# More three-pass blocks, eps in the Gram matrix, and small products spaced apart, in an attention and SwiGLU kernel

## The chip, the cores and the metric

The kernel runs on one core of a Trainium2 chip. The metric is the device time of one execution in microseconds, the median of several; executions of one kernel agree within some 0.3%. Every result was correct. Times of different jobs are compared through their ratios to the kernel before, which ran in each.

## The reference

```python
# x: 4 batches of 12416 tokens x 128 channels; 32 inducing points
h = mab(I, x); out = mab(x, h)        # mab: softmax attention, a = exp(s - max) / (sum + 1e-9), a @ kv
# then per token, 49664 tokens, d_ff = 1536
rms = sqrt(mean(out * out) + 1e-6); xn = out / rms * rms_g
g = xn @ w_gate; v = xn @ w_val
y = (g * sigmoid(g) * v) @ w_out
```

The second attention's division and the RMS norm need not both be done: with e the unnormalized weights and l their sum, out / rms is e·h / sqrt(mean((e·h)²) + 1e-6·l²). The kernel gets the mean from the Gram matrix of h, as eᵀ(hhᵀ)e / 128.

## The kernel before

Tokens go through the feed-forward part in units of up to 512, and each unit in twelve blocks of 128 columns of d_ff. A block is a gate matmul and a value matmul (into banks `gv`), a silu on ScalarE, a product `u` on VectorE, and a projection that adds to `acc`. Some blocks project in three reduced-precision passes instead of one full fp32 matmul; ScalarE and GpSimd prepare their operands:

```python
    def three(j, t):                      # what a three-pass block adds
        nc.scalar.activation(hi, v, AF.Copy, scale=1.0 - 2.0 ** -13)
        nc.gpsimd.tensor_tensor(out=lo, in0=v, in1=hi.bitcast(F32), op=ALU.subtract)
        ...                               # one block later:
        nc.scalar.activation(hs[:, 0:T], hi.bitcast(F32), AF.Copy, scale=2.0 ** -12)
        nc.gpsimd.tensor_tensor(out=d, in0=hs[:, 0:T], in1=lo.bitcast(F32), op=ALU.subtract)
```

Every 48 blocks a "seam" prepares the weights of the next four units, a step at a time between blocks. Its last step, `split`, turns the weights, rounds them (a cast) and takes the rest (a subtraction).

```python
        def split():
            aT = work.tile([P, 512], F32, name="aT", tag="work")
            nc.vector.transpose(out=aT[rows, 0:w], in_=sc[b][rows, cols2[s]])
            ...
            nc.vector.tensor_copy(out=hi[rows, 0:w], in_=aT[rows, 0:w])
            nc.vector.tensor_tensor(out=lo[rows, 0:w], in0=aT[rows, 0:w], in1=hi[rows, 0:w].bitcast(F32), op=ALU.subtract)
...
                # block of each seam step: turn_a, sum_l, square, turn_z, scale, apply, split
                j = ((14, 14, 17, 18, 21, 21, 33) if k else (32, 32, 33, 33, 34, 34, 37))[i]
```

All small products (scores, sums, the Gram product `square`) share one PSUM bank, `mm`. Before each exp, which occupies ScalarE (one instruction of 2.88 us at the first of a batch, two in 3.04 us at the second at 449 us, each with a table load of 1.28 us), the kernel holds projections back so that TensorE has work meanwhile.

## Time and profile before

| | before |
|---|---|
| median (range) | 1716.28 us (1715.45 to 1718.89) |
| profiled span, granted clock | 1713.4 us, 0.995 |
| TensorE busy | 98% |
| three-pass blocks | 337 of 1200 |

The prediction below shows the lines of the page and of the timeline, and how they are read. Two names recur. "Spacing" is the time from the start of one value matmul to the next, that is, the time of one block on TensorE. A "releaser" is what ended a wait.

### The profile page before, as it was taken

The page shows a single profiled execution, that of the slowest core. Times are in us where ns is not written, and L with a number is a line of the kernel's source. Part 1 is how long each engine was busy: PE and PEld are TensorE (multiplying, and loading weights), DVE is VectorE, ACT ScalarE, POOL GpSimd, SP SyncE. Part 2 cuts the span into 40 slices and gives each one's busy share as a digit, 9 for nine tenths or more (in the row PEclk, how much of TensorE's full clock was granted, in tenths as well). Part 3 has the DMA queues.
Part 4 walks back from the last instruction along what each step waited for, and adds up shares of the span by engine and source line. Part 5 has one row for each costly group of instructions (what it writes and reads, how often), then busy time and mean ns, then how long its engine had stood idle before and what let it go on. Part 6 is the DMA issues. An engine that isn't in the chain of part 4 may idle for free.

```text
span 1713.4 us, 23133 instructions
## 1 busy us (share of the span) xinstructions
PE 1676.4 (98%) x6791; PEld 1033.1 (60%) x6791; DVE 1203.1 (70%) x2086; ACT 1145.1 (67%) x2052; POOL 1029.4 (60%) x808
## 2 busy tenths in 40 slices
PE   9899999999999999999999999999999999999998
PEld 7545555655566656565556656566556666666666
DVE  4867876777677777667767787666767666766665
ACT  4346667665777676665667767766577777777775
POOL 0316663656477665465747766466647767767764
PEclk9899999999999999999999999999999999999999
DMA  6344433524343232434334313163211212121111
GB/s 248 87 68 74 73 76 61 120 64 73 60 79 68 48 61 56 102 73 93 64 55 82 67 34 81 31 131 75 59 30 32 39 31 37 31 38 34 35 36 24
DMA packets 389357, 112.64 MB, mean 66 GB/s; under 512 B 365136, under 2 KB 369776, under 8 KB 386672
## 3 DMA queue, kind: packets, MB, share of 16 engines
q1 hardware_dynamic: 388944, 111.02, 32.2%
q8 instruction: 54, 0.88, 0.2%
q14 instruction: 71, 0.58, 0.1%
q10 hardware_dynamic: 288, 0.15, 0.0%
HBM read 53.95 MB, written 27.00 MB: 47 GB/s over the span
## 4 chain that ended last, share of the span: by engine, by line
PE 88%; DVE 4%; ACT 4%; issue 2%; POOL 1%; DMA 1%; DVEq 0%; ACTq 0%; POOLq 0%
PE acc L555 43%; PE gv L604 15%; PE gv L602 15%; PE u L568 5%; PE u L570 4%; PE mm L300 2%; DVE u L608 1%; PE mm L483 1%; ACT silu L606 1%; PE mm L357 1%; DMA xn<-in_x_dram 1%; PE acc L177 1%; ACT sc L416 1%; ACT L606 1%; ACT sc L329 0%
## 5 line engine op out<-in xcount | busy, mean ns | idle before, releaser
L608 DVE TENSOR_TENSOR u<-silu,gv 128x512 f32<-128x512 f32 (+2 forms) x1200 | 787.8, 665 | 457.7 <-ACT silu L606 409.0
L606 ACT ACTIVATE silu<-gv 128x512 f32<-128x512 f32 (+2 forms) x1200 | 698.8, 584 | 491.2 <-PE gv L602 377.4
L555 PE MATMUL acc<-u,wo 128*128 128x512 f32 (+2 forms) x1726 | 863.1, 584 | 1.7 <-DVE u L608 1.0
L602 PE MATMUL gv<-a,sg 128*128 128x512 f32 (+2 forms) x1200 | 788.4, 657 | 7.7 <-ACT silu L606 5.3
L590 POOL TENSOR_TENSOR xn<-u,xn 128x512 fp32r<-128x512 f32 (+2 forms) x337 | 433.6, 1287 | 403.0 <-ACT xn L589 398.0
L604 PE MATMUL gv<-a,sv 128*128 128x512 f32 (+2 forms) x1200 | 469.4, 391 | 2.9 <-ACT silu L606 1.8
L595 POOL TENSOR_TENSOR xn<-hs,xn 128x512 fp32r<-128x512 f32 (+2 forms) x337 | 422.7, 1254 | 59.7 <-issue 15.9
L555 PEld LDWEIGHTS acc<-u,wo 128*128 128x128 f32 x1726 | 317.5, 189 | 112.9 <-issue 47.2
L602 PEld LDWEIGHTS gv<-a,sg 128*128 128x128 f32 x1200 | 227.2, 189 | 222.2 <-issue 151.0
L604 PEld LDWEIGHTS gv<-a,sv 128*128 128x128 f32 x1200 | 227.3, 189 | 216.0 <-issue 119.7
L589 ACT ACTIVATE xn<-u 128x512 fp32r<-128x512 f32 (+2 forms) x337 | 206.4, 612 | 20.7 <-DVE u L608 20.4
L594 ACT ACTIVATE hs<-xn 128x512 f32<-128x512 f32 (+2 forms) x337 | 206.3, 612 | 0.4 <-POOL xn L595 0.4
L568 PE MATMUL u<-xn,xn 128*128 128x512 f32 (+2 forms) x337 | 142.4, 422 | 0.0
L555 PE MATMUL acc<-xn,xn 128*128 128x512 f32 (+2 forms) x337 | 131.3, 390 | 2.8 <-POOL xn L595 2.8
L570 PE MATMUL u<-xn,xn 128*128 128x512 f32 (+2 forms) x337 | 130.6, 388 | 0.0
L498 POOL TENSOR_TENSOR rs<-ms,mhalf 128x16 f32<-128x16 f32 (+2 forms) x28 | 75.6, 2699 | 24.9 <-DVE ms L496 24.9
L568 PEld LDWEIGHTS u<-xn,xn 128*128 128x128 f32 x337 | 63.2, 188 | 27.2 <-issue 15.8
L490 POOL TENSOR_TENSOR z<-z,sc 128x512 f32<-128x512 f32 (+2 forms) x27 | 32.4, 1201 | 78.5 <-DVE z L489 47.3
L555 PEld LDWEIGHTS acc<-xn,xn 128*128 128x128 f32 x337 | 63.2, 188 | 18.1 <-POOL xn L595 4.3
L570 PEld LDWEIGHTS u<-xn,xn 128*128 128x128 f32 x337 | 63.4, 188 | 16.6 <-issue 4.3
L561 DVE STREAM_TRANSPOSE o<-o 128x512 f32<-128x512 f32 (+2 forms) x97 | 67.7, 698 | 3.4
L560 DVE TENSOR_TENSOR o<-acc,o 128x512 f32<-128x512 f32 (+2 forms) x97 | 64.7, 667 | 2.6 <-PE acc L555 2.2
(159 smaller groups left out, 789.1 us busy)
## 6 DMA issues: line engine op xcount, KB each, us to landing
out_dram<-o SPq DMA_DIRECT2D x320, 64.0 KB, 2.0
xT<-in_x_dram SPq DMA_DIRECT2D x60, 256.0 KB, 4.3
xn<-in_x_dram SPq DMA_DIRECT2D x60, 256.0 KB, 4.8
a<-hi SPq DMA_DIRECT2D x160, 64.0 KB, 2.0
a<-lo SPq DMA_DIRECT2D x158, 64.0 KB, 2.0
w<-w SPq DMA_DIRECT2D x22, 256.0 KB, 3.2
xn<-in_x_dram SPq DMA_DIRECT2D x5, 1024.0 KB, 10.6
out_dram<-o SPq DMA_DIRECT2D x64, 60.0 KB, 2.0
```

The costliest lines, as they stand in the source:

```text
L498: nc.gpsimd.tensor_tensor(out=rs, in0=ms, in1=mhalf[rows, 0:n], op=ALU.pow)
L555: nc.tensor.matmul(acc[:, 0:T], lhsT, rhs, start=st["left"] == NJ, stop=st["left"] == 1)
L568: nc.tensor.matmul(ups[:, 0:T], w[:, i, :], hi, start=st["k"] == nk, stop=False)
L570: nc.tensor.matmul(ups[:, 0:T], w[:, NK + i, :], lo, start=False, stop=not st["k"])
L589: nc.scalar.activation(hi, v, AF.Copy, scale=1.0 - 2.0 ** -13)
L590: nc.gpsimd.tensor_tensor(out=lo, in0=v, in1=hi.bitcast(F32), op=ALU.subtract)
L594: nc.scalar.activation(hs[:, 0:T], hi.bitcast(F32), AF.Copy, scale=2.0 ** -12)
L595: nc.gpsimd.tensor_tensor(out=d, in0=hs[:, 0:T], in1=lo.bitcast(F32), op=ALU.subtract)
L602: nc.tensor.matmul(g[:, 0:T], sg[:, ts(j, P)], a[:, 0:T], start=True, stop=True)
L604: nc.tensor.matmul(v[:, 0:T], sv[:, ts(j, P)], a[:, 0:T], start=True, stop=True)
L606: nc.scalar.activation(sl[:, 0:T], g[:, 0:T], AF.Silu)
L608: nc.vector.tensor_tensor(out=t[:, 0:T], in0=sl[:, 0:T], in1=v[:, 0:T], op=ALU.mult)
```

## The change

It means to save TensorE time (up to five blocks of twelve, instead of four, are projected in three passes), to take the sums of exponentials off VectorE (128·1e-6 added to every element of the Gram matrix yields the 1e-6·l² term), and to remove waits for the bank `mm`. It also holds one more projection back before exp.

```diff
-    KJ = range(0, NJ - 2, 3)
+    KJ = [j for j in range(NJ - 2) if j % 5 in (0, 2)] + [NJ - 3]
...
-    SLOT, SPLIT, RESERVE = 1.25, 2.9, 3
+    SLOT, SPLIT, RESERVE = 1.25, 2.75, 3
@@ Gram matrix
-                    nc.vector.tensor_copy(out=to, in_=of_)
+                    nc.vector.tensor_scalar_add(out=to, in0=of_, scalar1=C * 1e-6)
@@ seam
-        def sum_l():
-            l = st["l"] = numbers("l")
-            nc.vector.reduce_sum(out=l, in_=weights(b, s), axis=AX.X)
-            nc.vector.tensor_scalar_add(out=l, in0=l, scalar1=1e-9)
-            nc.vector.scalar_tensor_tensor(out=l, in0=l, scalar=1e-6, in1=l, op0=ALU.mult, op1=ALU.mult)
...
-            nc.vector.tensor_scalar(out=ms, in0=ms, scalar1=0.0, scalar2=1.0 / C, op0=ALU.max, op1=ALU.mult)
-            nc.vector.tensor_tensor(out=ms, in0=ms, in1=st["l"], op=ALU.add)
+            nc.vector.tensor_scalar(out=ms, in0=ms, scalar1=1.0 / C, scalar2=1e-6, op0=ALU.mult, op1=ALU.max)
@@ places of small products
-                at = 20 + 14 * s if b else 38 + 12 * s
+                at = 20 + 14 * s if b else 37 + 12 * s
...
-                add(199 + 7 * s, g["scores2"], s)
+                add(200 + 7 * s, g["scores2"], s)
...
-                add(175 + 18 * i, g["fetch"], i)
-                add(195 + 13 * i, g["stack"], i)
+                add(175 + 23 * i, g["fetch"], i)
+                add(197 + 7 * i, g["stack"], i)
@@ hold before exp
-                hold = k in held or any(k < e <= k + LAG - 2 for e in marks)
-                if hold and count < LAG - 1:
+                hold = k in held or any(k < e <= k + 3 for e in marks)
+                if hold and count < LAG:
...
-                spare = 1 if any(e <= k < e + LAG for e in marks) or (b, u) == flat[-1] else RESERVE
+                spare = 1 if any(e <= k < e + 4 for e in marks) or (b, u) == flat[-1] else RESERVE
```

Left out: the split of the output weights, which goes block by block since the positions are no longer evenly spaced, the same addition to the Gram matrix of the first batch, the transfers that follow the products at 197 and 204, and the renumbering that the missing step brings. From the seam on, a line number of the changed kernel is five or six lower than in the old one: the projection is L550, gate and value matmuls L597 and L599, silu L601, u L603, GpSimd's two subtractions L585 and L590, the Gram product L478, cast and subtraction of the split L502 and L503 (before: L508 and L509).

More of the change, by code (lines that the diff above doesn't have):

```diff
@@ L396, in square_h @@
                 if b:
-                    nc.vector.tensor_copy(out=to, in_=of_)
+                    nc.vector.tensor_scalar_add(out=to, in0=of_, scalar1=C * 1e-6)
                 else:
-                    nc.scalar.copy(out=to, in_=of_)
+                    nc.scalar.activation(to, of_, AF.Copy, bias=C * 1e-6)
         def scores2(s, ps=None):
@@ L509, in split @@
             nc.vector.tensor_tensor(out=lo[rows, 0:w], in0=aT[rows, 0:w], in1=hi[rows, 0:w].bitcast(F32), op=ALU.subtract)
-        return [turn_a, sum_l, square, turn_z, scale, apply, split]
+        return [turn_a, square, turn_z, scale, apply, split]
     def gather(b, u):
@@ L533, in split_wo @@
         whi, wlo, ws = (w[:, ts(k, NK), :] for k in range(3))
-        wk = wo[:, KJ.start:KJ.stop:KJ.step, :]
-        nc.vector.tensor_scalar_mul(out=whi, in0=wk, scalar1=1.0 - 2.0 ** -13)
-        nc.vector.tensor_tensor(out=wlo, in0=wk, in1=whi.bitcast(F32), op=ALU.subtract)
+        for i, j in enumerate(KJ):
+            nc.vector.tensor_scalar_mul(out=whi[:, i, :], in0=wo[:, j, :], scalar1=1.0 - 2.0 ** -13)
+        for i, j in enumerate(KJ):
+            nc.vector.tensor_tensor(out=wlo[:, i, :], in0=wo[:, j, :], in1=whi[:, i, :].bitcast(F32), op=ALU.subtract)
         nc.vector.tensor_scalar_mul(out=wlo, in0=wlo.bitcast(F32), scalar1=4096.0)
@@ L677 @@
     nc.scalar.activation(tiny[:], ones[:], AF.Silu)
-    turn_a, sum_l, square, turn_z, scale, apply, split = seam(0, 0)
+    turn_a, square, turn_z, scale, apply, split = seam(0, 0)
     turn_a()
     square()
-    sum_l()
     join(0, 1)
@@ L749, in schedule @@
             for i in range(2):
-                add(175 + 18 * i, g["fetch"], i)
-                add(195 + 13 * i, g["stack"], i)
+                add(175 + 23 * i, g["fetch"], i)
+                add(197 + 7 * i, g["stack"], i)
                 for k in range(R):
-                    add(197 + 13 * i + k, g["place"], i, k)
+                    add(199 + 7 * i + k, g["place"], i, k)
             add(254, g["exp2"], 0, NS)
@@ L772 @@
             for i, step in enumerate(seam(*one)):
-                j = ((14, 14, 17, 18, 21, 21, 33) if k else (32, 32, 33, 33, 34, 34, 37))[i]
+                j = ((14, 17, 18, 21, 21, 33) if k else (32, 33, 33, 34, 34, 37))[i]
                 n, j = divmod(j, NJ)
@@ L776 @@
                 seams.setdefault(at, []).append(step)
-                seam_busy[at] = seam_busy.get(at, 0) + {3: 1.4, 4: 3.0, 5: 1.2}.get(i, 0)
+                seam_busy[at] = seam_busy.get(at, 0) + {2: 1.4, 3: 3.0, 4: 1.2}.get(i, 0)
     flat = [(b, u) for b in range(B) for u in range(NU)]
```

## The prediction

> **What bounds the kernel now.** I began with the first and fourth parts of the page of the kernel before: busy time by engine, and the chain of work that ended last.
>
> ```profile
> PE 1676.4 (98%) x6791; PEld 1033.1 (60%) x6791; DVE 1203.1 (70%) x2086; ACT 1145.1 (67%) x2052; POOL 1029.4 (60%) x808
> ...
> PE 88%; DVE 4%; ACT 4%; issue 2%; POOL 1%; DMA 1%; DVEq 0%; ACTq 0%; POOLq 0%
> PE acc L555 43%; PE gv L604 15%; PE gv L602 15%; PE u L568 5%; PE u L570 4%; PE mm L300 2%; DVE u L608 1%; PE mm L483 1%; ACT silu L606 1%; PE mm L357 1%; DMA xn<-in_x_dram 1%; PE acc L177 1%; ACT sc L416 1%; ACT L606 1%; ACT sc L329 0%
> ```
>
> TensorE is busy 98% of the span and carries 88% of the chain. The granted clock is 0.995 in the profiled run, so the time is nearly what the matmuls cost, plus the few places where TensorE stops. Two numbers are therefore needed: what one block of the feed-forward part costs, and where it stops.
>
> For the first I read the timeline in the undisturbed last batch, and only starts, since matmul ends are modelled.
>
> ```profile
> 1400.79 0.39 PE L604 MATMUL gv<-a,sv 128*128 128x512 f32 x1
> ...
> 1400.85 1.29 POOL L590 TENSOR_TENSOR xn<-u,xn 128x512 fp32r<-128x512 f32 x1 [1.14 <-ACT xn L589]
> 1401.02 0.40 PE L568 MATMUL u<-xn,xn 128*128 128x512 f32 x1
> ...
> 1401.25 0.40 PE L570 MATMUL u<-xn,xn 128*128 128x512 f32 x1
> ...
> 1401.48 0.40 PE L555 MATMUL acc<-xn,xn 128*128 128x512 f32 x1
> ...
> 1401.95 0.39 PE L604 MATMUL gv<-a,sv 128*128 128x512 f32 x1
> ...
> 1402.19 1.02 PE L555 MATMUL acc<-u,wo 128*128 128x512 f32 x2
> 1402.29 1.28 POOL L595 TENSOR_TENSOR xn<-hs,xn 128x512 fp32r<-128x512 f32 x1
> ...
> 1403.28 0.39 PE L604 MATMUL gv<-a,sv 128*128 128x512 f32 x1
> ```
>
> From one L604 to the next, a block whose projection is in three reduced-precision passes takes 1401.95 - 1400.79 = 1.16 us, one whose projection is a full fp32 matmul 1403.28 - 1401.95 = 1.33 us; over many such pairs in this trace the medians are 1.16 and 1.32. Successive reduced passes start 0.23 us apart. So a three-pass block saves 0.16 us.
>
> For the second I asked for TensorE's own waits.
>
> ```profile
> PE gv L602 <- ACT silu L606: 5.3, 8, 1.0
> PE mm L483 <- DVE wlo L433: 4.4, 3, 1.5
> PE acc L555 <- POOL xn L595: 2.8, 3, 2.4
> PE mm L483 <- DVE sc L304: 2.6, 2, 1.5
> ...
> PE mm L429 <- PE gv L604: 1.9, 3, 0.6
> ```
>
> The columns are total us, times, longest. The five waits of L483 come to 7.0 us: this small product goes to the one PSUM bank called mm and must wait until VectorE has read out the product before it. The timeline of one shows it: L432 and L433 read the bank out at 383.91 to 385.3, and only then L483 starts, TensorE having been idle for 1.48 us.
>
> ```profile
> 385.45 1.04 PE L483 MATMUL mm<-eT,gram 128*128 128x480 f32 x2 [1.48 <-DVE wlo L433]
> ```
>
> L429 stands on TensorE just behind L604 (its releaser in the view), but at 360.38 VectorE was still copying the Gram matrix out of the same bank (0.79 us, itself late behind a GpSimd memset). It is the same kind of wait.
>
> [...] 1.32 less two passes of 0.23 leaves 0.86 us for the fp32 projection, 3.7 reduced passes, so three passes in place of it save less than a full one. [...]
>
> **The change part by part.** I counted instructions in the built programs, no time taken from them.
>
> Three passes. Blocks so treated go from 337 to 401: 55 more at width 512, 6 at 480, 3 at 256. At 0.16 us, scaled by width to 0.15 and 0.08, that is 8.8 + 0.9 + 0.2 = 9.9 us off TensorE, all on the path. Each adds two ScalarE copies of 0.62 us and two GpSimd subtractions of 1.29 and 1.28 us: 64 x 1.24 = 79 us and 64 x 2.57 = 165 us. ScalarE goes from 1145 to about 1224, GpSimd from 1029 to about 1194, some 72% and 70% of the new span. Beside other work, if they come in time.
>
> Spacing. The list of products on mm, by feed-forward block of a batch: before, L429 at 208 and L483 at 209 in three batches, now 204 and 209 with a score product between at 207. In the first batch, score products at 64 and 112 before L483 at 65 and 113; now at 63 and 111. These are exactly the five waits, so up to 7.0 us goes. The other L429 moves from 195 to 197, four blocks behind the Gram product at 193 rather than two: 1.9 us goes.
>
> Sums of exponentials. L475, L476, L477 and L496 go: about 0.64 + 3 x 0.17 = 1.2 us of VectorE in each of 28 seams, 33 us in all (the narrower ones are cheaper, so nearer 31). VectorE at 70% is no bound; I count only the 0.2 us of L496 before the first inverse root in the prologue. There the larger sum stands while TensorE runs its warm-up matmuls until 48.24 anyway. The addition to the Gram copy is one instruction for one.
>
> The backlog held for exp (count 5 for 4, plus a shorter release window). In the order of both programs the projections between the exp and the next gate matmul are the same six, two per block. So the main hole stays, 0.62 and about 1.0 us of TensorE idleness three times each. Only after the first kind does something change: a projection that waits for its u (block 138, 0.59 us late by the L604 spacing) is now one block later. 3 x 0.59 = 1.8 us.
>
> Sum: 9.9 + 7.0 + 1.9 + 1.8 + 0.2 = 20.8 us. Against it I set 1.5 us for new waits (below), an estimate by judgement. 1716.3 - 19.3 = 1697.0 us, 1.1% less.
>
> **The rivals.** First: GpSimd becomes late. In the old order three-pass blocks stand three apart, now pairs stand two apart, and 2 x 1.32 = 2.6 us is no more than the 2.57 us that GpSimd needs for one. The trace speaks mildly against it: the result above is ready at 1402.29 + 1.28 = 1403.57, and its pass is due five blocks after its u, at 1405.29, 1.7 us later. A second one that finds GpSimd busy loses some 0.15 us of that. In seams GpSimd also has 1.3 + 2.9 + 1.05 us of other work; the schedule there leaves blocks out, as it does now. The 2.4 us wait of L555 for L595 after the first exp (at 133) remains, for the order there is the same. If it did go wrong at one in four of the new blocks by 0.6 us, 64/4 x 0.6 = 10 us would be lost: 1706.
>
> Second: ScalarE becomes the bound locally. A unit of twelve blocks with five in three passes has 12 activations, 10 copies and one evacuation; at 0.5 us each when back to back (two silus take 1.09) that is 11.5 us of 7 x 1.32 + 5 x 1.16 = 15.0 us. Against it: 77% leaves room. For it: the copies come in bursts, and two pairs of gate banks are all the slack. If each of some 50 full units lost 0.2 us, it would be 10 us: again 1706.
>
> Third: the mm waits merely move, since the score product now at 207 is itself two blocks before L483. For it: the bank is still single. Against it: before, a product two blocks after a score product (206 to 208) shows no wait, and VectorE has lost its sums just there. If half of the 7 us stayed: 1700.
>
> Fourth: VectorE's relief pays more than I count, in the small waits for u around the seams (0.2 to 0.4 us, a dozen): perhaps 3 us more, 1694.
>
> **Range and chances.** The certain parts (passes, and most of the five waits) give 15 us; everything good gives 24, a rival gives back up to 10. I say 1690 to 1704. A gain of 2% is 34 us, more than all the parts together, and the losses would have to exceed 50 us for slower.
>
> **What would show it.** The block spacings of 1.16 and 1.32 must be unchanged; L483's waits for L433 and L304 gone; L429's wait gone; the exp holes as before; waits of TensorE for L595 under 5 us. It would be wrong if the three-pass spacing grew past 1.16 or if a wait for silu, L595 or L594 of over 5 us in sum stands newly in TensorE's list.

The sum is 20.8 us, less 1.5 us for new waits, which gives the 1697 us of the forecast.

## The result, and the profile after

The changed kernel took 1718.22 us in the median (1717.99 to 1719.31), the kernel before 1716.7 in the same rounds: ratio 1.0009, interval 0.9991 to 1.0026. The prediction was 1697, range 1690 to 1704.

First the page of the changed kernel, busy times and chain.

```profile
PE 1680.2 (98%) x6855; PEld 1045.7 (61%) x6855; DVE 1201.7 (70%) x1982; ACT 1207.7 (70%) x2180; POOL 1179.0 (69%) x936
...
PE 91%; ACT 3%; DVE 2%; issue 2%; DMA 1%; POOL 1%; ACTq 0%; DVEq 0%; POOLq 0%
```

One number is out of place. VectorE lost over a hundred instructions, some 31 us by my count, and its busy time fell by 1.4 us. (With the sums alone removed, in a run below, it fell by 28.7 us, from 1203.1 to 1174.4.) Something on VectorE became slower by 27 to 30 us. TensorE's own waits in the changed kernel (total us, times, longest):

```profile
PE gv L597 <- ACT silu L601: 6.6, 11, 1.0
PE gv L597 <- DVE u L603: 6.4, 11, 0.9
...
PE gv L599 <- DVE u L603: 3.3, 8, 0.8
PE acc L550 <- POOL xn L590: 2.4, 1, 2.4
...
PE mm L478 <- DVE eT L472: 0.9, 1, 0.9
```

The waits of the Gram product for other readers of `mm` are gone, as predicted, and GpSimd is not late: its one wait of 2.4 us stood in the kernel before too. What is new is waits for VectorE's `u`: 6.4 + 3.3 us where the kernel before had these:

```profile
PE gv L604 <- DVE u L608: 0.7, 3, 0.4
...
PE gv L602 <- DVE u L608: 0.4, 1, 0.4
```

Here is the place of one, in the last batch, where no small products other than the Gram product interfere. First the same place in the kernel before (start us, us, engine, line, operation):

```profile
1371.78 1.28 POOL L595 TENSOR_TENSOR xn<-hs,xn 128x512 fp32r<-128x512 f32 x1
...
1373.67 0.43 DVE L508 CAST hi<-aT 128x512 fp32r<-128x512 f32 x1
...
1374.14 0.69 DVE L509 TENSOR_TENSOR lo<-aT,hi 128x512 fp32r<-128x512 f32 x1
...
1374.22 1.76 POOL L590 TENSOR_TENSOR xn<-u,xn 128x512 fp32r<-128x512 f32 x1 [1.16 <-ACT xn L589]
```

The split fell into a gap of GpSimd's work. Its subtraction began 0.08 us ahead of GpSimd's next instruction, and that one took 1.76 us instead of 1.29. Now the changed kernel:

```profile
1372.60 1.30 POOL L590 TENSOR_TENSOR xn<-hs,xn 128x512 fp32r<-128x512 f32 x1
...
1373.19 0.98 DVE L502 CAST hi<-aT 128x512 fp32r<-128x512 f32 x1
...
1373.85 1.46 POOL L585 TENSOR_TENSOR xn<-u,xn 128x512 fp32r<-128x512 f32 x1
...
1374.21 1.66 DVE L503 TENSOR_TENSOR lo<-aT,hi 128x512 fp32r<-128x512 f32 x1
...
1375.39 1.60 POOL L590 TENSOR_TENSOR xn<-hs,xn 128x512 fp32r<-128x512 f32 x1
...
1376.52 0.50 PE L597 MATMUL gv<-a,sg 128*128 128x512 f32 x1 [0.65 <-DVE u L603]
```

With blocks 7 and 9 both in three passes, GpSimd has no gap at the split. Cast and subtraction each begin beside a running GpSimd instruction and take 0.98 and 1.66 us instead of 0.43 and 0.69. No `u` is made in between, the gate banks stay full, and TensorE stops for 0.65 us.

The view of one line gives all 28 splits (duration in ns: least, median, most; then first and last start). Kernel before, then changed kernel:

```profile
L508 DVE CAST hi<-aT x28: 282/427/1272, 56.8 to 1680.2; 128x512 fp32r<-128x512 f32 x20, 128x480 fp32r<-128x480 f32 x4, 32x256 fp32r<-32x256 f32 x4
...
L509 DVE TENSOR_TENSOR lo<-aT,hi x28: 411/693/1634, 57.3 to 1680.5; 128x512 fp32r<-128x512 f32 x20, 128x480 fp32r<-128x480 f32 x4, 32x256 fp32r<-32x256 f32 x4
```

```profile
L502 DVE CAST hi<-aT x28: 280/922/1236, 56.8 to 1682.8; 128x512 fp32r<-128x512 f32 x20, 128x480 fp32r<-128x480 f32 x4, 32x256 fp32r<-32x256 f32 x4
...
L503 DVE TENSOR_TENSOR lo<-aT,hi x28: 411/1613/1662, 57.3 to 1683.9; 128x512 fp32r<-128x512 f32 x20, 128x480 fp32r<-128x480 f32 x4, 32x256 fp32r<-32x256 f32 x4
```

The median cast doubled and the median subtraction more than doubled. That alone is 37.1 + 21.7 = 58.8 us against 21.1 + 15.6 = 36.7, so 22 of VectorE's missing 27 to 30 us.

In the changed kernel's trace 20 of the 28 subtractions begin within one of GpSimd's subtractions, and these take 1.32 to 1.66 us; the other eight begin with GpSimd idle and take 0.41 or 0.69. GpSimd is slowed too: its subtraction that began second, in the kernel before, took 1.76 us instead of 1.29. The trace shows the durations; what the two engines share it doesn't show.

To see where the time went I added up, in each trace, how far the spacing of every block exceeds what its matmuls cost undisturbed (1.32 us plain, 1.16 three-pass, plus the usual cost of a small product):

| stalls, us | before | after |
|---|---|---|
| Gram products, `mm` | 7.8 | -0.2 |
| product at 195 / 197 | 2.2 | 1.1 |
| split (blocks 35 to 38 of a seam) | 1.6 | 9.5 |
| narrow units and change of batch | 0.5 | 6.8 |
| first kind of exp, three times | 7.2 | 8.9 |
| second kind of exp, three times | 6.0 | 10.3 |
| all else | 16.4 | 18.5 |
| sum | 41.7 | 55.0 |

The sum rose by 13.2 us; the passes took off 9.9; net 3.3, and the two profiled spans differ by 3.2. The rows say where the time went, not yet why; that is for the experiments.

### The profile page after: what moved, and what is told of

Same layout as the page of the kernel before. It is cut to its first block, busy times and chain, and to the rows that moved or that the text cites. A ratio compares the mean times of both kernels' runs of the same rounds, so it can differ in the third digit from the quotient of the medians.

```text
span 1716.6 us, 23555 instructions
## 1 busy us (share of the span) xinstructions
PE 1680.2 (98%) x6855; PEld 1045.7 (61%) x6855; DVE 1201.7 (70%) x1982; ACT 1207.7 (70%) x2180; POOL 1179.0 (69%) x936
## 4 chain that ended last, share of the span: by engine, by line
PE 91%; ACT 3%; DVE 2%; issue 2%; DMA 1%; POOL 1%; ACTq 0%; DVEq 0%; POOLq 0%
PE acc L550 42%; PE gv L599 16%; PE gv L597 16%; PE u L563 5%; PE u L565 5%; PE mm L301 3%; ACT silu L601 1%; PE mm L478 1%; DVE u L603 1%; PE mm L358 1%; DMA xn<-in_x_dram 1%; PE acc L178 1%; ACT L601 1%; PE gv L358 0%; PE mm L430 0%
## 5 line engine op out<-in xcount | busy, mean ns | idle before, releaser
L603 DVE TENSOR_TENSOR u<-silu,gv 128x512 f32<-128x512 f32 (+2 forms) x1200 | 785.7, 665 | 444.6 <-ACT silu L601 378.3
L601 ACT ACTIVATE silu<-gv 128x512 f32<-128x512 f32 (+2 forms) x1200 | 699.5, 585 | 414.7 <-PE gv L597 357.9
L550 PE MATMUL acc<-u,wo 128*128 128x512 f32 (+2 forms) x1598 | 797.3, 583 | 0.1
L597 PE MATMUL gv<-a,sg 128*128 128x512 f32 (+2 forms) x1200 | 768.3, 640 | 14.6 <-ACT silu L601 6.6
L585 POOL TENSOR_TENSOR xn<-u,xn 128x512 fp32r<-128x512 f32 (+2 forms) x401 | 505.9, 1262 | 309.7 <-ACT xn L584 250.0
L590 POOL TENSOR_TENSOR xn<-hs,xn 128x512 fp32r<-128x512 f32 (+2 forms) x401 | 507.8, 1266 | 74.0 <-POOL xn L585 25.6
L599 PE MATMUL gv<-a,sv 128*128 128x512 f32 (+2 forms) x1200 | 475.7, 396 | 5.2 <-DVE u L603 3.3
L597 PEld LDWEIGHTS gv<-a,sg 128*128 128x128 f32 x1200 | 227.6, 190 | 223.4 <-issue 140.5
L599 PEld LDWEIGHTS gv<-a,sv 128*128 128x128 f32 x1200 | 228.1, 190 | 214.5 <-issue 125.7
L550 PEld LDWEIGHTS acc<-u,wo 128*128 128x128 f32 x1598 | 295.4, 189 | 93.5 <-issue 33.8
L584 ACT ACTIVATE xn<-u 128x512 fp32r<-128x512 f32 (+2 forms) x401 | 245.7, 613 | 17.6 <-DVE u L603 16.0
L589 ACT ACTIVATE hs<-xn 128x512 f32<-128x512 f32 (+2 forms) x401 | 246.3, 614 | 7.1 <-POOL xn L590 6.9
L563 PE MATMUL u<-xn,xn 128*128 128x512 f32 (+2 forms) x401 | 167.9, 419 | 0.0
L550 PE MATMUL acc<-xn,xn 128*128 128x512 f32 (+2 forms) x401 | 156.1, 389 | 2.4 <-POOL xn L590 2.4
L565 PE MATMUL u<-xn,xn 128*128 128x512 f32 (+2 forms) x401 | 155.4, 387 | 0.0
L563 PEld LDWEIGHTS u<-xn,xn 128*128 128x128 f32 x401 | 75.2, 188 | 43.2 <-issue 26.3
L565 PEld LDWEIGHTS u<-xn,xn 128*128 128x128 f32 x401 | 75.4, 188 | 19.1 <-issue 5.2
L550 PEld LDWEIGHTS acc<-xn,xn 128*128 128x128 f32 x401 | 75.3, 188 | 18.8 <-POOL xn L590 2.9
L555 DVE TENSOR_TENSOR o<-acc,o 128x512 f32<-128x512 f32 (+2 forms) x97 | 65.1, 671 | 21.7 <-ACT o L568 18.9
L568 ACT ACTIVATE o<-u 128x512 f32<-128x512 f32 (+2 forms) x97 | 56.4, 582 | 19.0 <-PE u L565 16.7
```

The lines of the kernel that those rows point to most:

```text
L550: nc.tensor.matmul(acc[:, 0:T], lhsT, rhs, start=st["left"] == NJ, stop=st["left"] == 1)
L563: nc.tensor.matmul(ups[:, 0:T], w[:, i, :], hi, start=st["k"] == nk, stop=False)
L565: nc.tensor.matmul(ups[:, 0:T], w[:, NK + i, :], lo, start=False, stop=not st["k"])
L597: nc.tensor.matmul(g[:, 0:T], sg[:, ts(j, P)], a[:, 0:T], start=True, stop=True)
L599: nc.tensor.matmul(v[:, 0:T], sv[:, ts(j, P)], a[:, 0:T], start=True, stop=True)
L601: nc.scalar.activation(sl[:, 0:T], g[:, 0:T], AF.Silu)
```

## The experiments

The theory, here the collision theory: the passes' gain is eaten because VectorE's cast and subtraction at the split take longer beside one of GpSimd's added subtractions (0.98 and 1.66 us for 0.43 and 0.69). The expectations call it the port theory; that is a name only, for no trace or run shows a port. That an operand in PSUM would spare them was a guess from `u`, which has one input there: it took at most 0.69 us in all 1200 blocks of the changed kernel, though over 500 of these began within a GpSimd subtraction. Rivals: the load of VectorE or ScalarE as such, the new hold, or the new spacing. Fourteen kernels ran, each five rounds against the kernel before. The last four are the changed kernel with the old hold put back; each of the last two builds on the one above it.

| run | median us | ratio (interval) |
|---|---|---|
| e1 passes alone | 1739.96 | 1.0138 (1.0124 to 1.0152) |
| e2 spacing alone | 1707.87 | 0.9948 (0.9936 to 0.9961) |
| e3 changed, split later | 1725.0 | 1.0048 (1.0034 to 1.0062) |
| e4 before, split one later | 1724.47 | 1.0045 (1.0032 to 1.0058) |
| e5 changed, old hold | 1713.57 | 0.9984 (0.9971 to 0.9996) |
| e7 sums alone | 1711.21 | 0.9971 (0.9957 to 0.9984) |
| e8 passes and sums | 1718.7 | 1.0013 (1.0001 to 1.0026) |
| e9 changed, PSUM operand | 1730.95 | 1.0084 (1.0070 to 1.0098) |
| e10 spacing and sums | 1705.87 | 0.9937 (0.9923 to 0.9950) |
| e11 changed, no passes at split | 1713.56 | 0.9979 (0.9966 to 0.9991) |
| b1 PSUM operand, split at 37, old hold | 1709.98 | 0.9961 (0.9949 to 0.9974) |
| b2 subtraction on GpSimd, old hold | 1701.69 | 0.9915 (0.9901 to 0.9928) |
| b3 and the cast on ScalarE | 1705.46 | 0.9935 (0.9923 to 0.9948) |
| b4 and all 401 blocks | 1706.4 | 0.9943 (0.9929 to 0.9957) |

**Passes alone.** The kernel before with the new KJ, the 2.75 and the split of the output weights.

```diff
-    KJ = range(0, NJ - 2, 3)
+    KJ = [j for j in range(NJ - 2) if j % 5 in (0, 2)] + [NJ - 3]
```

> The kernel before with the five-of-twelve passes alone (positions, split of the output weights, the scheduler's 2.75 us per block); old hold, old spacing, sums kept. Port theory (the two VectorE operations that split the weights of a seam, a cast and a subtraction of two SBUF tensors, are slowed by GpSimd's subtractions, which now run beside them): the cast takes 0.9 to 1.0 us and the subtraction 1.6 to 1.7 us in most of 28 seams, TensorE loses about 0.9 us after each of some 15, and the 9.9 us of the passes are nearly eaten: 1714 to 1719 us. Rival (the gain was lost elsewhere: in the hold, the new spacing, or by the sums' removal): the passes alone give their 9.9 us, about 1707 us.

1739.96 us: 24 us slower, beyond what even the collision theory had said. The cast and subtraction were as slow as in the changed kernel (0.93 and 1.62 us in the median). The surprise was one of the sums' tiny operations, the addition of 1e-9 to 128x16 numbers. In the kernel before, then here:

```profile
L476 DVE TENSOR_SCALAR l<-l x28: 158/174/493, 47.6 to 1657.1; 128x16 f32<-128x16 f32 x20, 128x15 f32<-128x15 f32 x4, 32x8 f32<-32x8 f32 x4
```

```profile
L476 DVE TENSOR_SCALAR l<-l x28: 157/1144/1295, 47.9 to 1678.8; 128x16 f32<-128x16 f32 x20, 128x15 f32<-128x15 f32 x4, 32x8 f32<-32x8 f32 x4
```

A median of 0.17 us became 1.14, nearly GpSimd's 1.28 us for a subtraction. That it ran beside one is my reading; the view gives durations alone. It stands just ahead of the read-out of `mm`, and the stalls at Gram products rose from 7.8 to 16.9 us.

**Spacing alone.** The kernel before with the block numbers of the diff (37, 200, 175 + 23i, 197 + 7i).

```diff
-                at = 20 + 14 * s if b else 38 + 12 * s
+                at = 20 + 14 * s if b else 37 + 12 * s
...
-                add(195 + 13 * i, g["stack"], i)
+                add(197 + 7 * i, g["stack"], i)
```

> The kernel before with the new block numbers of the small products alone. Both theories: L483's waits of 7.0 us and 1.1 to 1.9 us of L429 go, so 1707 to 1709 us; if the waits only move, 1714 us or more. The port theory expects the split operations as in the kernel before (0.43 and 0.69 us in most seams).

1707.87 us; 0.52% of 1716 is 8.9 us, which is 7.0 + 1.9 as read from the waits. The match is partly luck: by the spacing of the blocks, the Gram products lost all of their 7.8 us of stalls, and of the 2.2 us of the product at 195 half stayed as 0.4 us in each of three batches. The waits did not move elsewhere.

**Split later, in the changed kernel.**

```diff
-                j = ((14, 17, 18, 21, 21, 33) if k else (32, 33, 33, 34, 34, 37))[i]
+                j = ((14, 17, 18, 21, 21, 36) if k else (32, 33, 33, 34, 34, 37))[i]
```

> The changed kernel with the split of a seam three blocks later (36 for 33), where GpSimd stands still between the last three-pass block of a unit and the first of the next. Port theory: most casts back at 0.43 us, most subtractions at 0.69 us, the stalls of about 0.9 us at the split gone, 10 to 13 us less than the changed kernel: 1705 to 1709 us. Rival (the stall at the split comes from ScalarE's or VectorE's load, wherever the split stands): within 3 us of 1718.

A miss, outside both ranges: 1725.0 us, 7 us worse. The place was badly chosen. The casts were back at 0.43 us in the median, but the subtraction began just after GpSimd's next instruction:

```profile
1383.70 0.43 DVE L502 CAST hi<-aT 128x512 fp32r<-128x512 f32 x1
...
1384.02 1.28 POOL L585 TENSOR_TENSOR xn<-u,xn 128x512 fp32r<-128x512 f32 x1 [0.84 <-ACT xn L584]
1384.16 1.68 DVE L503 TENSOR_TENSOR lo<-aT,hi 128x512 fp32r<-128x512 f32 x1
```

It missed by 0.14 us and paid 1 us (1.68 for 0.69). The durations support the collision theory; the time doesn't test it, since the collision was only moved.

**Split one block later, in the kernel before.**

```diff
-                j = ((14, 14, 17, 18, 21, 21, 33) if k else (32, 32, 33, 33, 34, 34, 37))[i]
+                j = ((14, 14, 17, 18, 21, 21, 34) if k else (32, 32, 33, 33, 34, 34, 37))[i]
```

> The kernel before with its split one block later (34 for 33), so that it runs into GpSimd's subtraction, which in the kernel before began 0.08 us after it. Port theory: the cast or the subtraction (or both) takes about 1 us more in most seams and TensorE loses up to 0.9 us in each: 1720 to 1734 us. Rival: the split costs the same wherever it stands, within 2 us of 1716.7.

1724.47 us, as expected: with no pass and no instruction added, a shift by one block costs 0.45% or 7.7 us. The median subtraction took 1.48 us, the median cast 0.60, and the stalls at the split went from 1.6 to 9.5 us:

```profile
L509 DVE TENSOR_TENSOR lo<-aT,hi x28: 411/1479/1656, 57.4 to 1690.9; 128x512 fp32r<-128x512 f32 x20, 128x480 fp32r<-128x480 f32 x4, 32x256 fp32r<-32x256 f32 x4
```

More load can't be the reason here, for none was added.

**Old hold, in the changed kernel.** The three lines of the hold put back.

```diff
-                if hold and count < LAG:
+                if hold and count < LAG - 1:
```

> The changed kernel with the old hold before exp (4 pending for 5, the longer release). By the trace of the changed kernel the new hold makes TensorE run three gate pairs with nothing between them and wait for VectorE or ScalarE (0.65, 0.65, 0.42 us at the second exp of three batches, some 0.3 us at the first): expected 1 to 3 us less than the changed kernel, 1715 to 1717 us. If the hold is a gain as it was meant, 1719 us or more.

1713.57 us, better than the range of 1715 to 1717. Between the ratios lie 0.25 points, 4.3 us: the new hold loses time. (The two intervals still touch, 0.9996 and 0.9991; the executions, 1711.7 to 1716.8 and 1718.0 to 1719.3 us, do not.) To hold five back, TensorE runs three gate pairs with no projection between them, in the changed kernel here:

```profile
440.89 0.38 PE L599 MATMUL gv<-a,sv 128*128 128x480 f32 x1
...
441.32 0.38 PE L599 MATMUL gv<-a,sv 128*128 128x480 f32 x1
441.71 0.49 PE L597 MATMUL gv<-a,sg 128*128 128x480 f32 x1
...
442.40 0.48 PE L599 MATMUL gv<-a,sv 128*128 128x480 f32 x1 [0.20 <-DVE u L603]
```

Between the last two value matmuls lie 1.08 us instead of the 0.43 of the pair before, 0.20 of them spent waiting for VectorE's `u`, which empties the gate banks. The traces account for about 3 of the 4.3 us; about 1 goes with the granted clock, which averaged 0.9956 here and 0.9942 in the changed kernel (see "Clock" below).

**Sums alone.** The Gram and seam part of the diff on the kernel before.

```diff
-            nc.vector.tensor_scalar_add(out=l, in0=l, scalar1=1e-9)
...
-                    nc.vector.tensor_copy(out=to, in_=of_)
+                    nc.vector.tensor_scalar_add(out=to, in0=of_, scalar1=C * 1e-6)
```

> The kernel before with eps in the Gram matrix and the sums of exponentials gone, nothing else. VectorE loses some 30 us of work that lies beside TensorE, and its small operations did not collide with GpSimd there (0.17 us each): 1714 to 1717 us, the same. If the sums were on the path of L483 already, up to 5 us less.

1711.21 us, 5.0 us less: the second of the two expectations. The stalls at Gram products fell from 7.8 to 3.7 us, since the read-out of `mm` no longer queues behind the sums.

**Passes and sums together, old spacing and hold.** Both edits above.

```diff
-    KJ = range(0, NJ - 2, 3)
+    KJ = [j for j in range(NJ - 2) if j % 5 in (0, 2)] + [NJ - 3]
...
-            nc.vector.tensor_scalar_add(out=l, in0=l, scalar1=1e-9)
```

> The run of the passes alone, with the sums of exponentials removed as well (old spacing, old hold). Port theory: the run of the passes alone was 24 us slow partly because the addition of 1e-9 to the sums (0.18 us) took about 0.85 us in each seam behind GpSimd, on VectorE, ahead of the read-out that L483 waits for; without it L483's waits go back to about 7 us from 12 and the scattered stalls of 6 us go: 1720 to 1726 us. Rival (the sums do not matter, the passes themselves cost it): 1737 to 1741 us.

1718.7 us, 1.3 us better than the range. Beside the passes, the removal of the sums is worth 1.0138 - 1.0013, or 21 us; without them 5. The same edit has two prices: without the passes the addition that it removes took 0.17 us in the median, beside them 1.14.

**PSUM operand, in the changed kernel.** The cast then reads no SBUF and the subtraction one SBUF tensor.

```diff
-            aT = work.tile([P, 512], F32, name="aT", tag="work")
+            aT = ps_m.tile([P, 512], F32, name="mm", tag="mm")
```

> The changed kernel, with the transposed weights of a seam put in the PSUM bank mm instead of SBUF, so that the cast reads no SBUF at all and the subtraction only one SBUF tensor, as the product of silu and value does; same place in the order. Port theory: both take 0.65 to 0.70 us in all 28 seams whatever GpSimd does, GpSimd's subtractions stay at 1.29 us, the stalls at the split go: 1706 to 1711 us (up to 3 us of waits for the bank may be given back). Rival (VectorE's load at the split is what costs[...]): VectorE's time there falls little, 1716 us or more.

The durations did what the collision theory says, in every split (0.69 us at most for each):

```profile
L502 DVE CAST hi<-mm x28: 411/691/693, 56.7 to 1695.5; 128x512 fp32r<-128x512 f32 x20, 128x480 fp32r<-128x480 f32 x4, 32x256 fp32r<-32x256 f32 x4
...
L503 DVE TENSOR_TENSOR lo<-mm,hi x28: 411/691/693, 57.4 to 1696.0; 128x512 fp32r<-128x512 f32 x20, 128x480 fp32r<-128x480 f32 x4, 32x256 fp32r<-32x256 f32 x4
```

The time did not: 1730.95 us, by the number the rival's side. I had put a new user on the one bank that the change had just spread out, and TensorE waited for it:

```profile
PE mm L322 <- DVE lo L503: 7.8, 3, 2.6
...
PE mm L301 <- DVE lo L503: 4.0, 2, 2.0
```

Both are products one block after the split. The last batch has no such product, and there the comparison is clean. From the start of value matmul 912 to that of 1188 took 352.3 us before, 356.1 in the changed kernel and 350.2 here. The passes there went from 86 to 103; 17 x 0.16 = 2.7 us should be saved, and with the collision gone 2.1 are. With it, 3.8 are lost.

**Spacing and sums, without passes.** The edits of the two runs on the kernel before.

```diff
-                at = 20 + 14 * s if b else 38 + 12 * s
+                at = 20 + 14 * s if b else 37 + 12 * s
...
-            nc.vector.tensor_scalar_add(out=l, in0=l, scalar1=1e-9)
```

> The kernel before with the new spacing and without the sums, without the new passes and the new hold. The two alone gave 8.4 and 5.1 us, but both partly from L483's waits (7.8 us of stalls before; spacing leaves none of them): together 9 to 10.5 us, 1706 to 1708 us. If the two add up fully, 1703 us; if the new passes were worth anything in the full change, this kernel must be slower than the changed one's 1718 us.

1705.87 us, just under the range and 10.8 us less than before by the ratio. The two overlap, as both cure the same waits. This kernel is faster than the changed one, so the passes and the hold together cost time.

**No passes at the split, in the changed kernel.**

```diff
-            if (j not in KJ or b == 0 and u < 2 or ...
+            if (j in (7, 9) and (b, u, 9) in seams or j not in KJ or b == 0 and u < 2 or ...
```

> The changed kernel, in which the blocks 7 and 9 of the units that hold a seam's split keep the full fp32 projection, so that GpSimd has nothing to do while VectorE splits (361 three-pass blocks for 401). Port theory: cast 0.43 and subtraction 0.69 us in nearly all seams, the stalls at the split (some 12 us with those at the narrow units) gone, 40 x 0.16 = 6.4 us of passes given back: 1710 to 1715 us. Rival (GpSimd's presence is not what costs): 1718 + 6 = 1724 us.

1713.56 us: forty fewer three-pass blocks, and faster by 0.30 points, 5 us. Cast and subtraction are at 0.43 and 0.69 us in the median, and the stalls at the split are 0.2 us. The change also takes ScalarE's eighty copies for these blocks away, so this run alone doesn't part GpSimd from ScalarE. But it was VectorE's instructions that became fast again, and in the kernel before, with its split one block later, they had become slow with no change of load:

```profile
L503 DVE TENSOR_TENSOR lo<-aT,hi x28: 414/691/1632, 57.4 to 1677.6; 128x512 fp32r<-128x512 f32 x20, 128x480 fp32r<-128x480 f32 x4, 32x256 fp32r<-32x256 f32 x4
```

**PSUM operand with the split at 37, and the old hold.**

```diff
-                j = ((14, 17, 18, 21, 21, 33) if k else (32, 33, 33, 34, 34, 37))[i]
+                j = ((14, 17, 18, 21, 21, 37) if k else (32, 33, 33, 34, 34, 37))[i]
```

> The changed kernel with the old hold, the transposed weights in the PSUM bank, and the split at block 37 of a seam, at least two blocks from every product on that bank (at 33 it stood one block before products at 34, 130 and 178, which cost the run with the PSUM operand some 27 us). Port theory, with the bank as the only other cost: stalls at the split gone (some 8 to 10 us), no new waits for the bank, 4.6 us from the hold: 1699 to 1706 us, the passes' gain kept. Rival (something else eats the passes' gain): 1710 us or more.

1709.98 us, outside the collision theory's range and at the rival's edge of 1710. The split's stalls are gone (0.2 us), but 0.6 to 1.2 us per seam appear at blocks 40 and 41. There the value matmul waits for ScalarE's silu:

```profile
1375.64 0.50 PE L599 MATMUL gv<-a,sv 128*128 128x512 f32 x1 [0.29 <-ACT silu L601]
```

Shortly before, at 1372.98, ScalarE had waited 0.78 us for a `u` that stood on VectorE behind the split's three instructions, 2.1 us in a row. So VectorE's time at the split counts also without a collision. That reading comes from the trace; no run isolates it.

**Subtraction on GpSimd, and the old hold.** On GpSimd the subtraction only stands in line with GpSimd's others, and the scheduler, told of it, leaves out 18 three-pass blocks (383). `engine` is GpSimd in all seams but the first.

```diff
-            nc.vector.tensor_tensor(out=lo[rows, 0:w], in0=aT[rows, 0:w], in1=hi[rows, 0:w].bitcast(F32), op=ALU.subtract)
+            engine.tensor_tensor(out=lo[rows, 0:w], in0=aT[rows, 0:w], in1=hi[rows, 0:w].bitcast(F32), op=ALU.subtract)
...
-                seam_busy[at] = seam_busy.get(at, 0) + {2: 1.4, 3: 3.0, 4: 1.2}.get(i, 0)
+                seam_busy[at] = seam_busy.get(at, 0) + {2: 1.4, 3: 3.0, 4: 1.2, 5: 1.3}.get(i, 0)
```

> The changed kernel with the old hold and the seam's subtraction moved to GpSimd (1.3 us there, told to the scheduler, which then leaves 383 three-pass blocks). Port theory: the subtraction can't collide any more, the cast still takes 0.9 to 1.0 us; VectorE's time at the split falls from 3.4 to 1.7 us and most of the stall goes: 1704 to 1712 us. Rival: 1714 us or more.

1701.69 us, ratio 0.9915: better than the range and the fastest of all, faster than both kernels, though by less than 2%. The cast stayed slow, 0.94 us in the median. The split's stalls are 1.2 us, those of the narrow units 2.5. Against the run with the old hold alone that is 0.69 points, 12 us. The run mixes two edits, the engine and the 18 blocks; the last run below keeps all 401 and is still 0.41 points, 7 us, better than that one, but it moves the cast too.

**Cast on ScalarE as well, and all blocks.** First with the same 383 three-pass blocks, then with the scheduler not told of the 1.3 us, so with 401.

```diff
-            nc.vector.tensor_copy(out=hi[rows, 0:w], in_=aT[rows, 0:w])
+            nc.scalar.copy(out=hi[rows, 0:w], in_=aT[rows, 0:w])
```

> The run with the subtraction on GpSimd, with the cast moved to ScalarE too (383 three-pass blocks, old hold). If the collisions are all that is left, the remaining stalls at the split and the narrow units (some 3.7 us by slot spacing) go: 1697 to 1701 us. Rival (ScalarE is the tighter engine, its 28 more copies of 0.6 us delay the silus): 1702 us or more.

> The same with the scheduler not told of GpSimd's 1.3 us, so with all 401 three-pass blocks. If GpSimd keeps up, 18 x 0.16 = 2.9 us less than the run before it, 1695 to 1699 us; if GpSimd is late, TensorE waits for its subtraction (L590) by more than the 2.4 us that it does now, and the run is the slower of the two, 1701 us or more.

1705.46 us, the rival's side: to take the last collision away costs more than it saves. In TensorE's waits of the 383-block run, the waits for silu grew from 6.5 to 8.3 us:

```profile
PE gv L597 <- ACT silu L601: 8.3, 14, 1.0
```

Three of them are new, at block 131 of three batches (0.95 us of stall for 0.38), two blocks after a split, where ScalarE copies ahead of a silu. With 401 blocks it took 1706.4 us, no better: TensorE's wait for GpSimd stayed at 2.4 us, so GpSimd is not late in that sense, but the stalls at the split rose from 2.3 to 4.6. Neither of the two outcomes occurred. The trace shows what differs at a split of the last batch. With 401 blocks ScalarE's copy for the added pass stands between two silus:

```profile
1367.98 0.59 ACT L601 ACTIVATE silu<-gv 128x512 f32<-128x512 f32 x1
...
1368.47 0.62 ACT L584 ACTIVATE xn<-u 128x512 fp32r<-128x512 f32 x1
...
1368.99 0.59 ACT L601 ACTIVATE silu<-gv 128x512 f32<-128x512 f32 x1
```

With 383 the two silus follow each other (1.08 us for both, at 1365.34). The next `u` starts 1.01 us after the one before it, and TensorE waits 0.14 us for it, at six of the splits. So here ScalarE, which was given the cast, is the tight engine; that is read from the order, and no run tests it.

## Why the prediction was wrong

The parts, as the runs price them in ratios of about 1716 us: spacing and sums -10.8 us; the passes added to these, with the old hold, +8.1 (0.9937 to 0.9984); the new hold +4.3 (to 1.0009). Sum: +1.6 us, the change's result.

- **Spacing.** Predicted -7.0 and -1.9, measured -8.9 alone. Right in size, the exact match by luck (7.8 and 1.1 by the spacing of blocks), and so was the rejection of the rival that the waits would move.
- **Three passes.** The step that failed is the sentence "Beside other work, if they come in time." The cost on TensorE was right: median spacings stayed at 1.16 and 1.33 us, and their 9.9 us stand in the accounting. GpSimd came in time as well; its one wait of 2.4 us did not grow. But I asked only whether GpSimd's added 165 us would be late, not what they would slow. They slowed VectorE's cast and subtraction at the split by 22 us, and the stalls at the splits and narrow units rose by 14. The passes brought +8 us instead of -9.9. None of my four rivals had this in it. GpSimd late: TensorE's waits for its result went from 2.8 to 2.4 us. ScalarE as the bound: the gate and value matmuls' waits for silu went from 7.1 to 7.7 us. The bank: the five waits of the Gram product for other readers were gone. What grew were their waits for `u`, from 1.1 to 9.7 us, and `u` was not on my list of what would show me wrong.
- **Sums.** Counted as 0.2 us on the path. Alone they were worth 5.0, since they stood on VectorE ahead of the read-out that the Gram product waits for; beside the passes 21, since their tiny addition took 1.14 us there instead of 0.17. My fourth rival (VectorE's relief pays 3 us more) had the direction, though it looked for it in the waits for `u`. I judged them by VectorE's share of busy time rather than by their place.
- **The hold.** I said that the hole around exp stays; it does (0.98 and about 1.38 us of stall where there were 1.03 and 1.41). The gain of 3 x 0.59 us at block 138 did not come: the wait became one of 0.72 us. And I read the order only from the exp onwards, not the blocks in which the fifth projection is saved up. The term of -1.8 measured +4.3.
- **Clock.** I took it as given. In the changed kernel's profile, TensorE had two more stretches of 3.4 us at a granted clock of 0.50 after its start than before (three, at 136, 453 and 1280 us, for one, at 868 us, the last few microseconds aside). Two stand in the exp rows of the table, where before had one; the third is at 136 us. No run shows that the change brings them about. Over the 107 executions, each compared with the mean of its kernel in its job, 0.001 less granted clock went with 0.8 us more (correlation -0.81). By this estimate the clock has about 1 us in the hold's 4.3, and about 4 in the 21 us by which the sums' removal helps beside the passes (0.9918 without it, 0.9966 with it).

What stays open: why the clock differs between kernels. And the passes fell short by 18 us (+8.1 for -9.9), of which the stalls at splits and narrow units are 14; about 4 us have no cause shown. Nor did any run collect the passes' full 9.9 us: the best kernel has 383 - 337 = 46 more three-pass blocks than the run with spacing and sums alone, worth 46 x 0.16 = 7.4 us, and is 3.8 us faster by the ratios.

## What to carry to other kernels

Work moved to an engine with time to spare has to be checked for what it slows on its neighbours, not only for whether it is done in time: here, with GpSimd subtractions of 1.28 us added, a VectorE cast took 0.98 us for 0.43, a two-input subtraction 1.66 for 0.69 and a small addition 1.14 for 0.17. A schedule tuned to a gap of 0.08 us breaks when anything around it moves, so look in the trace of before for pairs that just miss each other. If an engine's busy time fails to fall when its instructions go, compare the median duration of each line first.

## Two measurements besides

- The slow clock. In the changed kernel's profile it came after a stop of 0.97 us within a stretch where TensorE was busy 14.82 of 16 us; the mean granted clock (after the busy times in the lines below) was 0.66 from 452 to 457 us. A stop of 1.00 us at the same place in the kernel before kept the full clock (1.00 from 448 to 462 us, busy 13.00 of 14), so its length alone doesn't decide it.

```profile
441.00:457.00 16.00, 14.82 (x42) 7.74 (x40) 7.58 (x14) 11.97 (x16) 1.45 (x3) 0.89 0.24 41
452.00:457.00 5.00, 5.00 (x12) 2.56 (x12) 4.04 (x8) 2.56 (x5) 1.30 (x2) 0.66 0.31 45
```

- GpSimd's power took 2.7 us on average for at most 128x16 numbers, twice its subtraction of 128x512 (1.29 and 1.28 us).
